# Two row tiles for the 448-deep products, four rotating PSUM bank pairs, and num/den between the halves

## The chip, the cores and the metric

The kernel runs on one core of one Trainium2 chip. The metric is the device time of one execution in microseconds. Executions of one kernel fall into a fast and a slow state; only fast ones are compared. The kernel before took 162.58 us (median of four runs, 162.56 to 162.85).

Names used below: PE is the matmul engine, ACT the scalar engine, DVE the vector engine, POOL the general one, SP the engine that issues most DMAs.

## The reference, cut to what matters

```python
xn  = layernorm(x)                                  # x: 2048 x 448
q, k, v = split(xn @ wqkv)                          # 16 heads of 28
phi = lambda p: concat(softmax(p), softmax(-p))     # p = q or k times w_phi, per head
kv  = einsum(phi(k), v);  z = sum(phi(k))
attn = (phi(q) @ kv) / (phi(q) @ z + 1e-6) @ wo     # "num / den"
ffn  = mish(xn @ w1 + b1) @ w2                      # 448 -> 1792 -> 448
out  = x + attn + ffn
```

Every product with `xn` or the attention output has a contraction of 448 = 7 x 64. The array has 128 rows, so 448 is three and a half passes.

## The kernel before

A 448-deep operand is stored as four chunks of 128 rows that overlap in one 64-row stretch. Of two outputs, each gets three 128-row products (`full`), and then both get their last 64 rows in one go: one output on the array's lower half, the other on the upper half (`rem`, "a half pair").

```python
C0 = (0, 128, 192, 320);  HP = 64;  FULL = ((0, 2, 3), (0, 1, 3))
def full(e, out, lhs, rhs, u, start=True, stop=False):
    for n, c in enumerate(FULL[u]):
        i = e.matmul(out, lhs(ALLP, c), rhs(ALLP, c), start=(start and n == 0), stop=(stop and n == 2))
def rem(e, out, lhs, rhs, u, start=False, stop=True):
    h = slice(HP * u, HP * (u + 1))
    return e.matmul(out, lhs(h, 1 + u), rhs(h, 1 + u), start=start, stop=stop)
```

In the projections one step handles one pair of row tiles (j) and one block of q (i). v alternates between PSUM banks 0-1 and 2-3, k always uses 4-5, q always 6-7, and ACT empties them (`kexp`, `qexp`: two exponentials each, `vevac`: a copy; DVE copies the last two v).

```python
def proj(j, i):
    # v(j): full, full ; q(i): full, full, rem -> qexp ; v(j): rem ; k(j): rem
    # (j == 0: transposes of xn; j == 1: the products that make Wpq)
    # k(j): full, full -> kexp(j), vevac(j)
```

In the FFN stage, two blocks n and n+1 (each 128 columns of w1 for 1024 tokens) share one stretch of half pairs, and num/den products of two token tiles follow it (56 rows deep; no extra step shows between them and half pairs):

```python
for n in range(2 * FC):
    ffn1_full(n, 0); ffn1_full(n, 1)
    ms = [m for m in (n - ND0, n - ND0 + 1) if n % 2 == 0 and 0 <= m < NT]      # ND0 = 8
    if n % 2 == 0:
        ffn1_rem(n)                     # half pairs of n and n + 1
        for m in ms: nd_mm(m)           # num and den on PE, banks 4-5 or 6-7
    mish(n)
    for m in ms: nd(m)                  # five DVE instructions, one POOL product and a small copy
    # ... kv_mm and kvz at n = 0, 2, 4 ; transposes of the attention output
```

The softmax here doesn't subtract the row's maximum and nothing guards it: scores larger than these inputs give would overflow.

## Time and profile before

| what | value | where it is read |
|---|---|---|
| span | 161.0 us | page |
| PE busy, modelled | 95% | page, engines |
| 128-row products, start to start | 216 ns (512 wide), 189 ns (448 wide) | timeline |
| half pairs, start to start | the same 216 and 189 ns | timeline |
| extra per change of array form | about 96 ns, 56 times (54 between 128-row and 64-row forms, 2 from the 56-column kv sums to 128-column products) | timeline |
| ACT per projection step, back to back | 4.37 us | timeline, 25 to 42 us |
| DVE per num/den tile | 1.955 us | timeline, 71 to 97 us |

Columns of the page's first lines: engine, busy us, share of the span, instructions; then one digit for each fortieth of the span, in tenths.

```profile
PE 153.0 (95%) x1317; PEld 75.9 (47%) x1317; DVE 81.8 (51%) x173; ACT 73.2 (45%) x78; POOL 57.4 (36%) x75
...
PE   6999999999799899999999999999999999999992
...
DVE  0877999993449604079999999000051210005211
ACT  3558898999957944655555555620000000000000
```

PE looks full nearly everywhere, which says little: the ends of its matmuls are modelled. The Trainium skill (Perfetto Trace Analysis, Identifying the Most-Contended Engine) says as much, that matmul occupancy is no measure of the distance to the roofline. What counts is from start to start. The next view is the timeline of PE in the FFN stage: start, length, engine, line, operation, output and inputs, array rows x columns, size, count.

```profile
65.02 0.61 PE L348 MATMUL PS<-xnT,W 64*128 64x512 bf16 x4
65.56 2.76 PE L343 MATMUL PS<-xnT,W 128*128 128x512 bf16 x12
68.26 0.60 PE L348 MATMUL PS<-xnT,W 64*128 64x512 bf16 x4
```

Twelve products at 216 ns are 2.59 us, but the half pairs start 2.70 us after the first of the twelve. Two half pairs at 216 ns are 0.43 us, but the twelve start 0.54 us after them. So each change of form costs about 0.1 us. The Trainium skill (TensorEngine Tiling (Array Packing), Key Properties) names the reason: a change of tiling mode drains the engine. It gives no size; this trace does.

The second loss is in the projections. An idle time of the engine stands in brackets with what ended it.

```profile
40.48 1.47 PE L343 MATMUL PS<-xnT,Wpq 128*128 128x512 bf16 x6 [0.42 <-ACT EqT L440]
...
44.31 1.47 PE L343 MATMUL PS<-xnT,Wpq 128*128 128x512 bf16 x6 [0.79 <-ACT EqT L440]
```

q has one bank pair, so these q products wait for the exponentials of the q before. From start to start PE loses 0.58 and 0.96 us here; the brackets show less, since modelled ends overlap the wait.

The third limit is DVE. In the chain of waits (start, length, what), the whole stretch from 69 to 96 us reads like this (steps of 0.02 us named "issue" are left out):

```profile
70.98 0.25 DVE rden L505
71.24 0.12 DVE rq L500
71.38 0.19 DVE rq L501
71.59 0.65 DVE t_1 L503
72.27 0.65 DVE t_1 L504
72.94 0.25 DVE rden L505
```

The last instruction of one tile starts at 70.98 and that of the next at 72.94: DVE needs 1.955 us per token tile, PE with its switches about 1.85.

### The profile page before, as it was taken

How to read it: one execution, taken by the hardware profiler on the slowest of the kernel's cores; microseconds unless marked ns; L12 is line 12 of the kernel's file. 1: busy time of each engine (PE TensorE's matmuls, PEld its weight loads, DVE VectorE, ACT ScalarE, POOL GpSimd, SP SyncE). 2: the span in 40 equal slices, each digit the busy share in tenths (PEclk: the TensorE clock that was granted, in tenths of full speed). 3: DMA queues.
4: the chain of work that ended last, by engine and by line, in shares of the span. 5: the costliest groups of instructions: out<-in, count | busy, mean ns of one | idle time of the engine just before them, and what ended most of it. 6: DMA issues, size and time to landing. Idle time of an engine off the chain costs nothing.

```text
span 161.0 us, 3133 instructions
## 1 busy us (share of the span) xinstructions
PE 153.0 (95%) x1317; PEld 75.9 (47%) x1317; DVE 81.8 (51%) x173; ACT 73.2 (45%) x78; POOL 57.4 (36%) x75
## 2 busy tenths in 40 slices
PE   6999999999799899999999999999999999999992
PEld 6854334443246355344444444455545555545550
DVE  0877999993449604079999999000051210005211
ACT  3558898999957944655555555620000000000000
POOL 6223489977435970026666666300000000000000
PEclk9999999999999999999999999999999999999999
DMA  5995994337910000003336336300022000003010
GB/s 134 328 178 187 280 289 50 67 69 172 372 35 4 0 6 4 0 0 65 69 68 69 66 65 69 65 0 0 0 81 65 29 29 31 4 0 114 29 57 29
DMA packets 24414, 12.79 MB, mean 79 GB/s; under 512 B 17936, under 2 KB 23760, under 8 KB 24400
## 3 DMA queue, kind: packets, MB, share of 16 engines
q1 hardware_dynamic: 23760, 11.65, 30.5%
q10 hardware_dynamic: 608, 0.94, 1.6%
q8 instruction: 10, 0.16, 0.4%
q14 instruction: 4, 0.03, 0.1%
q0 software_dynamic: 32, 0.00, 0.0%
HBM read 6.62 MB, written 1.84 MB: 53 GB/s over the span
## 4 chain that ended last, share of the span: by engine, by line
PE 57%; DVE 24%; ACT 13%; POOL 2%; issue 2%; POOLq 0%; DVEq 0%
PE PS L558 26%; PE PS L343 21%; ACT EqT L440 7%; PE PS L348 4%; ACT hm L419 3%; DVE stats L276 3%; DVE t_0 L504 3%; DVE t_1 L504 3%; DVE t_0 L503 3%; DVE t_1 L503 3%; PE PS L615 2%; DVE rden L505 2%; DVE xn L289 2%; DVE rq L501 2%; ACT v_ext L601 2%
## 5 line engine op out<-in xcount | busy, mean ns | idle before, releaser
L558 PE MATMUL PS<-W,hm 128*128 128x448 bf16 x224 | 44.8, 352 | 0.0
L543 ACT ACTIVATE hm<-PS,b1T 128x1024 bf16<-128x1024 f32 x28 | 31.2, 1113 | 20.9 <-PE PS L343 13.7
L343 PE MATMUL PS<-xnT,W 128*128 128x512 bf16 x168 | 39.0, 380 | 0.6 <-ACT hm L543 0.6
L566 DVE TENSOR_TENSOR out_sb<-PS,x_all 128x448 bf16<-128x448 f32 x16 | 9.4, 621 | 48.8 <-PE PS L348 29.9
L558 PEld LDWEIGHTS PS<-W,hm 128*128 128x128 bf16 x224 | 21.9, 98 | 20.5
L432 POOL TENSOR_TENSOR hm<-hm,rSk 128x1792 bf16<-128x1792 bf16 x8 | 25.6, 3210 | 8.6 <-DVE rSk L431 8.6
L343 PEld LDWEIGHTS PS<-xnT,W 128*128 128x128 bf16 x168 | 15.2, 98 | 19.4 <-issue 1.6
L440 ACT ACTIVATE EqT<-PS 128x1024 bf16<-128x1024 f32 x16 | 15.5, 1021 | 4.6 <-PE PS L348 4.6
L425 DVE TENSOR_REDUCE Sk<-hm 128x64 f32<-128x1792 bf16 x8 | 15.8, 1981 | 0.0
L508 POOL TENSOR_TENSOR o_sb<-t_0,rden 128x504 bf16<-128x504 f32 x8 | 8.3, 1038 | 16.4 <-DVE rden L505 16.4
L419 ACT ACTIVATE hm<-PS 128x896 bf16<-128x896 f32 x16 | 13.9, 927 | 0.3 <-PE PS L343 0.2
L343 PE MATMUL PS<-xnT,Wpq 128*128 128x512 bf16 x48 | 11.7, 379 | 1.2 <-ACT EqT L440 1.2
L343 PE MATMUL PS<-Wo,EqT 128*128 128x448 bf16 x48 | 11.7, 353 | 0.0
L343 PE MATMUL PS<-Wv,xnT 128*128 128x448 bf16 x48 | 10.6, 353 | 0.7 <-DMA xnT<-xn 0.4
L276 DVE BATCH_NORM_STATS2 stats<-x_all 128x6 f32<-128x448 bf16 x16 | 9.3, 616 | 3.7 <-DMA x_all<-in_A_x_dram 3.7
L343 PE MATMUL PS<-Wpk,xnT 128*128 128x448 bf16 x48 | 10.5, 354 | 0.0
L508 POOL TENSOR_TENSOR o_sb<-t_1,rden 128x504 bf16<-128x504 f32 x8 | 8.3, 1039 | 5.3 <-DVE rden L505 5.3
L289 DVE TENSOR_SCALAR xn<-x_all,mv,rstd 128x512 bf16<-128x512 bf16 x16 | 7.3, 497 | 2.4 <-POOL rstd L284 2.3
L348 PE MATMUL PS<-xnT,W 64*128 64x512 bf16 x56 | 8.5, 381 | 0.0
L343 PEld LDWEIGHTS PS<-xnT,Wpq 128*128 128x128 bf16 x48 | 4.5, 98 | 7.0 <-ACT EqT L440 2.1
L343 PEld LDWEIGHTS PS<-Wv,xnT 128*128 128x128 bf16 x48 | 4.2, 98 | 5.5 <-DMA xnT<-xn 0.8
L343 PEld LDWEIGHTS PS<-Wo,EqT 128*128 128x128 bf16 x48 | 4.5, 98 | 4.8 <-issue 0.7
(67 smaller groups left out, 131.7 us busy)
## 6 DMA issues: line engine op xcount, KB each, us to landing
W<-in_B_w_dram SPq DMA_DIRECT2D x2, 896.0 KB, 5.9
out_dram<-out_sb SPq DMA_DIRECT2D x16, 112.0 KB, 1.7
W<-in_B_w_dram SPq DMA_DIRECT2D x1, 1568.0 KB, 7.1
x_all<-in_A_x_dram SPq DMA_DIRECT2D x4, 224.0 KB, 4.4
x_all<-in_A_x_dram ACTq DMA_DIRECT2D x1, 896.0 KB, 5.2
Wv<-in_A_wqkv_dram SPq DMA_DIRECT2D x2, 224.0 KB, 4.5
Wo<-in_A_wo_dram SPq DMA_DIRECT2D x2, 224.0 KB, 6.9
Wk<-in_A_wqkv_dram SPq DMA_DIRECT2D x2, 196.0 KB, 3.6
```

The costliest lines, as they stand in the source:

```text
L276: dve(lambda v: v.bn_stats(stats[:, t, :], x_all[:, t, :]), r=[f"x{t}"], w=[f"st{t}"])
L289: eng(lambda v: v.tensor_scalar(xn[i][:, t % 2, :].rearrange("p (a b) -> p a b", a=2), ap_on(x_all[:, t, 0:1], [[192, 2], [1, 256]]), mv[: ...
L343: i = e.matmul(out, lhs(ALLP, c), rhs(ALLP, c), start=(start and n == 0), stop=(stop and n == 2))
L348: return e.matmul(out, lhs(h, 1 + u), rhs(h, 1 + u), start=start, stop=stop)
L419: act(lambda a, s=s: a.activation(Ek[j % 4][:, :, s, :], PS[:, 4:6, 0:D], ACT.Exp, scale=(1.0 if s == 0 else -1.0)), w=[f"Ek{j % 4}{s}"], ...
L425: dve(lambda v: v.tensor_reduce(Sk[b][:, :], Ek[q][:, :, :, :].rearrange("p t s (h f) -> p (t s h) f", f=DH), AX.X, ALU.add), r=[f"Ek{q}0" ...
L432: pool(lambda g: g.tensor_tensor(phik[:, 2 * j:2 * j + 2, :].rearrange("p t (k f) -> p (t k) f", f=DH), Ek[q][:, :, :, :].rearrange("p t s ...
L440: act(lambda a, s=s: a.activation(EqT[:, s, 2 * gp:2 * gp + 2, tc * 512:(tc + 1) * 512], PS[:, 6:8, :], ACT.Exp, scale=(1.0 if s == 0 else ...
L503: dve(lambda v: v.tensor_tensor(t2v, ps(1, 0, E1), rho, ALU.mult), r=[f"rho{i}"], w=[f"t2{i}"], x=[b, b + 1])
L508: pool(lambda g: g.tensor_tensor(ap_on(ot[:, 0:1], [[KC * P - hh_, 2], [DH, 9], [1, DH]]), ap_on(t1[i][:, 0, 0:1], [[7 * E1, 2], [E1, 9], ...
L543: act(lambda a: a.activation(hm[tcp][:, fc, :].rearrange("p (u n) -> p u n", u=2), PS[:, b:b + 2, :], ACT.Mish, bias=b1T[:, fc:fc + 1]), r ...
L558: i = e.matmul(PS[:, bs[u], cs], hm[q][:, fc, u * P:(u + 1) * P], W2[:, fc, :], start=(u < 4 and fc == 0), stop=(u >= 4 and fc == FC - 1))
```

## The change

The intent is to keep PE in one array mode through the projections, the FFN and the num/den products. Every pair of 448-deep products becomes seven half pairs, except v and k of the first two row tiles, which keep the old form: in half pass `a` output 0 takes the lower half of four chunks while output 1 takes the upper half; in half pass `b` the roles change for the other three. Two row tiles must not write one PSUM bank at the same time (the Trainium skill, TensorEngine Tiling (Array Packing), Gotcha 1: PSUM Pressure), so `b` waits on PE's own semaphore until `a` is done (`fence`), and another block or the num/den products stand between the two.

```diff
+    class Blk:
+        def a(self):
+            def f(e):
+                for c in range(KC):
+                    self.mm(e, 0, LO, c, c == 0, False)
+                    i = self.mm(e, 1, HI, c, c == 0, False)
+                return i
+            self.fence = pe(f, r=self.r, x=self.banks)
+        def b(self):
+            def f(e):
+                for n in range(3):
+                    self.mm(e, 1, LO, (0, 1, 3)[n], False, n == 2)
+                    i = self.mm(e, 0, HI, (0, 2, 3)[n], False, n == 2)
+                return i
+            pe(f, x=self.banks, fence=self.fence)
+            self.done()
+    def two(X, Y):
+        X.a(); Y.a(); X.b(); Y.b()
+    BA, BB, BC, BE = (0, 1), (2, 3), (6, 7), (4, 5)
+    vbank = [BA, BB, BB, BA, BE, BC, BB, BA]
+    kbank = [BE, BE, BC, BB, BA, BE, BC, BB]
+    qbank = [BA, BE, BC, BB, BA, BE, BC, BA]
     ... (v, k, q, FFN and Wo products become Blk; proj, ffn1_full, ffn1_rem, final go)
+    def fbank(n):
+        if n < 6:
+            return (BB, BC, BA)[n % 3]
+        if n < 22:
+            return (BB, BA)[n % 2]
+        return (BE, BB, BA, BC, BE, BB)[n - 22]
     ... (main sequence)
-        if j < 2:
-            wload("SP", W1[:], B_w1, "W1", (j,))
+        if j in (2, 3):
+            wload("SP", W1[:], B_w1, "W1", (j - 2,))
+    two(Q(0), V(2)); two(K(2), Q(1)); two(V(3), K(3)); two(Q(2), V(4)); two(K(4), Q(3))
+    two(V(5), K(5)); two(Q(4), V(6)); two(K(6), Q(5)); two(V(7), K(7)); two(Q(6), Q(7))
     ... (kv_mm(0..3); FF 0,1; kv_mm(4,5); FF 2,3; kv_mm(6,7), kvz; FF 4,5)
+    for n in range(6, 22):
+        X = FF(n)
+        X.a()
+        nd_mm(n - 6)
+        X.b()
+        nd(n - 6)
+        oTr(n - 6)
+    for n in (22, 24, 26):
+        two(FF(n), FF(n + 1))
     ... (last stage: Wo in four groups of half passes, between them the 14 products per tile with W2)
```

More of the change, by code (lines that the diff above doesn't have):

```diff
@@ L51, in __init__, with add @@
         self.dmas = []
-    def add(self, eng, fn, r=(), w=(), x=(), dma=False):
+    def add(self, eng, fn, r=(), w=(), x=(), dma=False, fence=None):
         st = self.streams[eng]
@@ L81, in add @@
                 best[o.eng] = o
+        if fence is not None and known.get(eng, -1) < fence.idx:
+            best[eng] = fence
         for key, o in list(best.items()):
@@ L377, in sl @@
         return lambda h, c: w[h, c, :]
-    VB = (0, 2)
-    def vargs(j, u):
-        t = 2 * j + u
-        return PS[:, VB[j % 2] + u, 0:D], xs(t, 1), sl(Wv)
-    def kargs(j, u):
-        t = 2 * j + u
-        return PS[:, 4 + u, 0:D], xs(t, 1), sl(Wpk)
-    def qargs(i, u):
-        tc, gp = i // 2, i % 2
-        g = 2 * gp + u
-        return PS[:, 6 + u, :], sl(Wpq[:, :, g, :]), xs(4 * tc, 4)
-    def proj(j, i):
-        vb = VB[j % 2]
-        for u in range(2):
-            pe(lambda e, u=u: full(e, *vargs(j, u), u), r=[f"xT{j}"] + wk("Wv"), x=[vb + u])
-        if i is not None:
-            for u in range(2):
-                pe(lambda e, u=u: full(e, *qargs(i, u), u),
-                   r=[f"xT{2 * (i // 2)}", f"xT{2 * (i // 2) + 1}", "Wp000", "Wp001", "Wp010", "Wp011", "Wpq_pad"], x=[6 + u])
-            pe(lambda e: (rem(e, *qargs(i, 0), 0), rem(e, *qargs(i, 1), 1))[1], x=[6, 7])
-            qexp(i // 2, i % 2)
-        pe(lambda e: (rem(e, *vargs(j, 0), 0), rem(e, *vargs(j, 1), 1))[1], x=[vb, vb + 1])
-        pe(lambda e: (rem(e, *kargs(j, 0), 0, True, False), rem(e, *kargs(j, 1), 1, True, False))[1],
-           r=["Wp100", "Wp110"], x=[4, 5])
-        if j == 0:
-            xT_pe(1, act)
-        if j == 1:
-            w_mm(0, 0, 6, dve)
-            w_mm(0, 1, 0, act)
@@ new lines, in _kernel, with __init__, mm @@
+    LO, HI = slice(0, HP), slice(HP, P)
+    class Blk:
+        def __init__(self, outs, lhs, rhs, banks, r, done, start=True, stop=True):
+            self.outs, self.lhs, self.rhs, self.banks, self.r, self.done = outs, lhs, rhs, banks, r, done
+            self.start, self.stop = start, stop
+        def mm(self, e, u, h, c, start, stop):
+            return e.matmul(self.outs[u], self.lhs[u](h, c), self.rhs[u](h, c), start=start and self.start,
+                            stop=stop and self.stop)
+        def a(self):
[13 more added lines that the diff above has]
+            self.done()
@@ new lines, in two, with bk, V @@
+    def two(X, Y):
+        X.a()
+        Y.a()
+        X.b()
+        Y.b()
+    BA, BB, BC, BE = (0, 1), (2, 3), (6, 7), (4, 5)
+    vbank = [BA, BB, BB, BA, BE, BC, BB, BA]
+    kbank = [BE, BE, BC, BB, BA, BE, BC, BB]
+    qbank = [BA, BE, BC, BB, BA, BE, BC, BA]
+    def bk(bs, n):
+        return [PS[:, b, 0:n] for b in bs]
+    def V(j):
+        return Blk(bk(vbank[j], D), [xs(2 * j, 1), xs(2 * j + 1, 1)], [sl(Wv)] * 2, list(vbank[j]),
+                   [f"xT{j}"] + wk("Wv"), lambda: vevac(j))
@@ new lines, in K, with Q @@
+    def K(j):
+        return Blk(bk(kbank[j], D), [xs(2 * j, 1), xs(2 * j + 1, 1)], [sl(Wpk)] * 2, list(kbank[j]),
+                   [f"xT{j}", "Wp100", "Wp110"], lambda: kexp(j))
+    def Q(i):
+        tc, gp = i // 2, i % 2
+        return Blk(bk(qbank[i], 512), [sl(Wpq[:, :, 2 * gp + u, :]) for u in range(2)], [xs(4 * tc, 4)] * 2,
+                   list(qbank[i]), [f"xT{2 * tc}", f"xT{2 * tc + 1}", "Wp000", "Wp001", "Wp010", "Wp011", "Wpq_pad"],
+                   lambda: qexp(tc, gp))
@@ new lines, in first @@
+    def first():
+        vb, kb = vbank[0], kbank[0]
+        va = [(PS[:, vb[u], 0:D], xs(u, 1), sl(Wv)) for u in range(2)]
+        ka = [(PS[:, kb[u], 0:D], xs(u, 1), sl(Wpk)) for u in range(2)]
+        for u in range(2):
+            pe(lambda e, u=u: full(e, *va[u], u), r=["xT0"] + wk("Wv"), x=[vb[u]])
+        pe(lambda e: (rem(e, *va[0], 0), rem(e, *va[1], 1))[1], x=list(vb))
+        vevac(0)
+        pe(lambda e: (rem(e, *ka[0], 0, True, False), rem(e, *ka[1], 1, True, False))[1],
+           r=["Wp100", "Wp110"], x=list(kb))
+        pe(lambda e: e.transpose(PSb[:, 6, 0:FC], b1_rows[0:FC, :], ident[0:FC, 0:FC]), r=["b1r", "ident"], x=[6])
+        xT_pe(1, act)
@@ L412, in proj @@
         for u in range(2):
-            pe(lambda e, u=u: full(e, *kargs(j, u), u, False, True), r=[f"xT{j}", "Wp100", "Wp110"], x=[4 + u])
-        kexp(j)
-        vevac(j)
+            pe(lambda e, u=u: full(e, *ka[u], u, False, True), r=["Wp100", "Wp110"], x=[kb[u]])
+        kexp(0)
     def kexp(j):
+        b = kbank[j]
         for s in range(2):
-            act(lambda a, s=s: a.activation(Ek[j % 4][:, :, s, :], PS[:, 4:6, 0:D], ACT.Exp,
-                                            scale=(1.0 if s == 0 else -1.0)), w=[f"Ek{j % 4}{s}"], x=[4, 5])
+            act(lambda a, s=s: a.activation(Ek[j % 4][:, :, s, :], PS[:, b[0]:b[0] + 2, 0:D], ACT.Exp,
+                                            scale=(1.0 if s == 0 else -1.0)), w=[f"Ek{j % 4}{s}"], x=list(b))
@@ L438, in qexp @@
     def qexp(tc, gp):
+        b = qbank[2 * tc + gp]
         for s in range(2):
             act(lambda a, s=s: a.activation(EqT[:, s, 2 * gp:2 * gp + 2, tc * 512:(tc + 1) * 512],
-                                            PS[:, 6:8, :], ACT.Exp, scale=(1.0 if s == 0 else -1.0)),
-                w=[f"Eq{tc}{gp}{s}"], x=[6, 7])
+                                            PS[:, b[0]:b[0] + 2, :], ACT.Exp, scale=(1.0 if s == 0 else -1.0)),
+                w=[f"Eq{tc}{gp}{s}"], x=list(b))
     def kv_mm(j):
@@ L517, in oTr, with FF @@
         dma_t("SP", oT[:, :, t * P:(t + 1) * P], o_sb[t % NO][:], r=[f"o{t % NO}", f"oa{t % NO}"], w=[f"oT{t}"])
-    def fargs(n, u):
-        tcp, fc = n // FC, n % FC
-        return PS[:, 2 * (n % 2) + u, :], sl(W1[:, :, fc * P:(fc + 1) * P]), xs(8 * tcp + 4 * u, 4)
-    def ffn1_full(n, u):
-        tcp = n // FC
-        first = n % 2 == 0
-        pe(lambda e: full(e, *fargs(n, u), u, first, not first),
-           r=wk("W1") + [f"xT{4 * tcp + 2 * u}", f"xT{4 * tcp + 2 * u + 1}"], x=[2 * (n % 2) + u])
-    def ffn1_rem(n):
-        for i in (n, n + 1):
-            pe(lambda e, i=i: (rem(e, *fargs(i, 0), 0, i > n, i == n), rem(e, *fargs(i, 1), 1, i > n, i == n))[1],
-               r=wk("W1") + [f"xT{4 * (i // FC) + u}" for u in range(4)], x=[2 * (i % 2), 2 * (i % 2) + 1])
+    def fbank(n):
[4 more added lines that the diff above has]
+        return (BE, BB, BA, BC, BE, BB)[n - 22]
+    def FF(n):
+        tcp, fc = n // FC, n % FC
+        b = fbank(n)
+        return Blk(bk(b, 512), [sl(W1[:, :, fc * P:(fc + 1) * P])] * 2, [xs(8 * tcp + 4 * u, 4) for u in range(2)],
+                   list(b), wk("W1") + [f"xT{4 * tcp + u}" for u in range(4)], lambda: mish(n))
     def mish(n):
         tcp, fc = n // FC, n % FC
-        b = 2 * (n % 2)
+        b = fbank(n)
         if tcp:
@@ L542, in mish @@
             rr = [f"Ek{i}{u}" for i in range(4) for u in range(2)]
-        act(lambda a: a.activation(hm[tcp][:, fc, :].rearrange("p (u n) -> p u n", u=2), PS[:, b:b + 2, :], ACT.Mish,
-                                   bias=b1T[:, fc:fc + 1]), r=["b1T"], w=[f"hm{tcp}"] + rr, x=[b, b + 1])
-    OB = [5, 6, 7, 4, 0, 1, 2, 3]
-    def final(q):
-        ts = [8 * q + u for u in range(8)]
-        bs = [OB[u] for u in range(8)]
-        cs = slice(0, D)
-        def wo(u):
-            return PS[:, bs[u], cs], sl(oT[:, :, ts[u] * P:(ts[u] + 1) * P]), sl(Wo)
-        def f1(e, u):
+        act(lambda a: a.activation(hm[tcp][:, fc, :].rearrange("p (u n) -> p u n", u=2), PS[:, b[0]:b[0] + 2, :],
+                                   ACT.Mish, bias=b1T[:, fc:fc + 1]), r=["b1T"], w=[f"hm{tcp}"] + rr, x=list(b))
@@ L557, in f1, with WO, f @@
+    OB = [0, 1, 6, 7, 4, 5, 2, 3]
+    def WO(t, first):
+        bs = [OB[(t + u) % 8] for u in range(2)]
+        return Blk(bk(bs, D), [sl(oT[:, :, (t + u) * P:(t + u + 1) * P]) for u in range(2)], [sl(Wo)] * 2, bs,
+                   [f"oT{t + u}" for u in range(2)] + wk("Wo"), lambda: None, start=first, stop=not first)
+    def f1(t, first):
+        q, u, bank = t // 8, t % 8, OB[t % 8]
+        def f(e):
             for fc in range(FC):
-                i = e.matmul(PS[:, bs[u], cs], hm[q][:, fc, u * P:(u + 1) * P], W2[:, fc, :],
-                             start=(u < 4 and fc == 0), stop=(u >= 4 and fc == FC - 1))
@@ L560, in f1 @@
-            return i
-        def evac(u):
-            t = ts[u]
-            i = t % 4
-            key = f"out{i}"
-            dve(lambda v: v.tensor_tensor(out_sb[i][:, :], PS[:, bs[u], cs], x_all[:, t, :], ALU.add),
-                r=[f"x{t}"], w=[key], x=[bs[u]])
-            dma("SP", ov[:, t, :], out_sb[i][:, :], r=[key])
-        for u in range(4):
-            pe(lambda e, u=u: f1(e, u), r=[f"hm{q}", "W2"], x=[bs[u]])
-            pe(lambda e, u=u: full(e, *wo(u), u % 2, False, False), r=[f"oT{ts[u]}"] + wk("Wo"), x=[bs[u]])
@@ L573, in final @@
-        for v in range(4):
-            pe(lambda e, v=v: [rem(e, *wo(2 * v + u), u, v >= 2, v < 2) for u in range(2)][1],
-               r=[f"oT{ts[2 * v + u]}" for u in range(2)], x=bs[2 * v:2 * v + 2])
-        for u in range(4):
-            evac(u)
-        for u in range(4, 8):
-            pe(lambda e, u=u: full(e, *wo(u), u % 2, False, False), x=[bs[u]])
-            pe(lambda e, u=u: f1(e, u), x=[bs[u]])
-            evac(u)
+                i = e.matmul(PS[:, bank, 0:D], hm[q][:, fc, u * P:(u + 1) * P], W2[:, fc, :],
+                             start=(first and fc == 0), stop=(not first and fc == FC - 1))
@@ L583, in _kernel, with evac @@
+            return i
+        pe(f, r=[f"hm{q}", "W2"], x=[bank])
+    def evac(t):
+        i = t % 4
+        dve(lambda v: v.tensor_tensor(out_sb[i][:, :], PS[:, OB[t % 8], 0:D], x_all[:, t, :], ALU.add),
+            r=[f"x{t}"], w=[f"out{i}"], x=[OB[t % 8]])
+        dma("SP", ov[:, t, :], out_sb[i][:, :], r=[f"out{i}"])
     NP = NT // 2
@@ L594, in vevac @@
     def vevac(j):
-        vb = VB[j % 2]
+        vb = vbank[j]
         out = v_ext[:, 2 * j:2 * j + 2, :, 0:DH]
-        src = PS[:, vb:vb + 2, 0:D].rearrange("p t (h d) -> p t h d", d=DH)
+        src = PS[:, vb[0]:vb[0] + 2, 0:D].rearrange("p t (h d) -> p t h d", d=DH)
         if j >= 6:
-            dve(lambda v: v.tensor_copy(out, src), w=[f"v{j}"], x=[vb, vb + 1])
+            dve(lambda v: v.tensor_copy(out, src), w=[f"v{j}"], x=list(vb))
         else:
-            act(lambda a: a.activation(out, src, ACT.Copy), w=[f"v{j}"], x=[vb, vb + 1])
+            act(lambda a: a.activation(out, src, ACT.Copy), w=[f"v{j}"], x=list(vb))
     def ln_a(j):
@@ L616, in warm @@
            r=["ident"], x=[7])
-    def qlast(i):
-        tc = i // 2
-        for u in range(2):
-            pe(lambda e, u=u: full(e, *qargs(i, u), u),
-               r=[f"xT{2 * tc}", f"xT{2 * tc + 1}", "Wp000", "Wp001", "Wp010", "Wp011", "Wpq_pad"], x=[6 + u])
-        pe(lambda e: (rem(e, *qargs(i, 0), 0), rem(e, *qargs(i, 1), 1))[1], x=[6, 7])
-        qexp(tc, i % 2)
     warm(28)
@@ L642, in _kernel, with after @@
     ln_a(2)
-    for j in range(NP):
-        proj(j, j - 2 if 2 <= j <= 6 else 6 if j == 7 else None)
-        if j == 6:
-            qlast(5)
+    def after(j):
         if j == 0:
+            dve(lambda v: v.tensor_copy(b1T[:], PSb[:, 6, 0:FC]), w=["b1T"], x=[6])
             ln_b(2)
@@ L650, in _kernel @@
             ln_a(3)
-        else:
-            if j >= 2:
-                knorm(j - 2)
-            if j == 1:
-                ln_b(3)
-                xT(3)
-            if j + 3 < NP:
-                ln_a(j + 3)
-            if 1 < j < NP - 2:
-                ln_b(j + 2)
-                xT(j + 2)
-            if j >= 2:
-                knorm2(j - 2)
-        if j < 2:
-            wload("SP", W1[:], B_w1, "W1", (j,))
+            return
+        if j >= 2:
+            knorm(j - 2)
+        if j == 1:
+            ln_b(3)
+            xT(3)
+        if j + 3 < NP:
+            ln_a(j + 3)
+        if 1 < j < NP - 2:
+            ln_b(j + 2)
+            xT(j + 2)
+        if j >= 2:
+            knorm2(j - 2)
+        if j in (2, 3):
+            wload("SP", W1[:], B_w1, "W1", (j - 2,))
         elif j == 5:
@@ L670, in _kernel @@
             masks()
-        if j == 2:
-            pe(lambda e: e.transpose(PSb[:, 3, 0:FC], b1_rows[0:FC, :], ident[0:FC, 0:FC]), r=["b1r", "ident"], x=[3])
-            dve(lambda v: v.tensor_copy(b1T[:], PSb[:, 3, 0:FC]), w=["b1T"], x=[3])
-    ffn1_full(0, 0)
-    ffn1_full(0, 1)
-    qlast(7)
+    first()
+    after(0)
+    V1, K1 = V(1), K(1)
+    V1.a()
+    w_mm(0, 0, 0, dve)
+    w_mm(0, 1, 6, act)
+    K1.a()
+    V1.b()
+    K1.b()
+    after(1)
+    two(Q(0), V(2))
+    after(2)
+    two(K(2), Q(1))
+    two(V(3), K(3))
+    after(3)
+    two(Q(2), V(4))
+    after(4)
+    two(K(4), Q(3))
+    two(V(5), K(5))
+    after(5)
+    two(Q(4), V(6))
+    after(6)
+    two(K(6), Q(5))
+    two(V(7), K(7))
+    after(7)
+    two(Q(6), Q(7))
     knorm(NP - 2)
@@ L680, in _kernel @@
     knorm2(NP - 1)
-    KV_END = 4
-    ND0 = 8
-    for n in range(2 * FC):
-        if n:
-            ffn1_full(n, 0)
-            ffn1_full(n, 1)
-        ms = [m for m in (n - ND0, n - ND0 + 1) if n % 2 == 0 and 0 <= m < NT]
-        if n == 0:
-            for j in range(4):
-                kv_mm(j)
-        if n % 2 == 0:
-            ffn1_rem(n)
-            for m in ms:
-                nd_mm(m)
-        mish(n)
-        for m in ms:
-            nd(m)
-        if n == 2:
-            kv_mm(4)
-            kv_mm(5)
-        if n == KV_END:
-            kv_mm(6)
-            kv_mm(7)
-            kvz()
-        for m in ms:
-            oTr(m)
-    for q in range(2):
-        final(q)
+    for j in range(4):
+        kv_mm(j)
+    two(FF(0), FF(1))
+    kv_mm(4)
+    kv_mm(5)
+    two(FF(2), FF(3))
+    kv_mm(6)
+    kv_mm(7)
+    kvz()
+    two(FF(4), FF(5))
+    for n in range(6, 22):
+        X = FF(n)
+        X.a()
+        nd_mm(n - 6)
+        X.b()
+        nd(n - 6)
+        oTr(n - 6)
+    for n in (22, 24, 26):
+        two(FF(n), FF(n + 1))
+    two(WO(0, True), WO(2, True))
+    for t in range(4):
+        f1(t, False)
+        evac(t)
+    two(WO(4, True), WO(6, True))
+    two(WO(8, True), WO(10, True))
+    for t in range(4, 9):
+        f1(t, False)
+        evac(t)
+    two(WO(12, True), WO(14, True))
+    for t in range(9, 16):
+        f1(t, False)
+        evac(t)
     pr.finish()
```

## The prediction

> **What bounds the kernel now.** Span 161.0 us (162.57 us timed), clock 1.0. The page gives PE 95% busy, but matmul ends are modelled, so I read start-to-start times in the timeline. Full 128-row products follow each other every 216 ns (512 wide) or 189 ns (448 wide); two 64-row products on different halves start 3 ns apart and such pairs follow at the same 216 or 189 ns. Seven half pairs cost what six full products plus one half pair cost: no gain in array time. Removed:
>
> 1. *Mode switches.* Going from 128-row to 64-row products the next start comes 312 ns after the last instead of 216; coming back 308 ns, then 226. About 96 ns per switch, which agrees with the Trainium skill, TensorEngine Tiling (Array Packing), Key Properties: a change of tiling mode drains the engine. The trace holds 56 switches (about 5.3 us). By the new order I count 16; 40 x 0.096 = 3.8 us.
> 2. *Bank waits in the projections.* PE waits 0.58, 0.96 and 0.72 us (at 40.5 and 44.3 on the q exponentials through the single q bank pair, at 55.1 on the Mish), 0.43 us for b1T at 23.0, 0.56 us for an xnT transpose at 17.4. Rotation should remove most: about 2.5 us.
>
> **Added or moved.** A fence on PE's own semaphore between halves: the other block (0.76-0.86 us) or num/den products (0.22 us) between should hide it. The Wpq products now stand before most of V1 and all of K1. They cannot start before 14.8 us (the last WTq load lands at 14.67, DMA issues); about 0.5 us is lost.
>
> **By stage.** Projections: ACT needs 4.37 us per pair of row tiles (0.92+0.90 q, 2x0.80 k, 0.95 v; back to back from 25 to 42), PE 4.17 + 0.19 switch. Both are nearly full, so switches alone gain little; ACT starves from 42 to 51 while PE waits. After: first q exponential near 19.9, then 28.0 us of ACT work, last q product on PE near 46 (was 50.6). FFN blocks 0 and 1 are complete near 51 (was 54.4): -3.4 us.
>
> FFN1: each num/den tile costs DVE 1.955 us against PE 1.85 per tile now; the chain of waits is DVE from 69.1 to 96.4. Switches removed inside this loop gain nothing. But the loop starts after 6.6 blocks instead of 10, at about 60.5 instead of 69.1; six FFN blocks then run at 1.51 us instead of four at 1.62. The phi_k products on POOL (3.21 us each) end near 55.4 and become co-critical for the last kv sums. FFN1 ends near 98.2 (was 104.7). Final stage: 53.4 us either way.
>
> **Predicted:** 161.0 - 6.4 = 154.6 span, 156.2 us; range 153.3 to 159.4. Faster by over 2% (below 159.3) 0.88, within 2% 0.10, slower 0.02.
>
> **What would show it.** Half pairs every 216/189 ns in long runs; no 312 ns steps in FFN1; the q waits gone and ACT continuous from about 20 to 48 us; first num/den near 60 us, DVE still 1.955 us per tile with PE waiting on it; start of the FFN2 products about 6 us earlier, the last 56 us unchanged.
>
> **What would make it wrong.** Half pairs in long runs slower than 216 ns (doubled weight loads not hidden); a fence wait at each half; ACT or the xnT transposes holding PE in the rotated projections; phi_k late, so the kv sums stall and the whole DVE loop moves later. Each costs 1-4 us; only slower pairs could undo the gain.

## The result, and the profile after

The changed kernel took 157.31 us (157.18 to 158.14, four runs) against 162.58. The ratio is 0.9683, with a 95% interval of 0.9648 to 0.9718. A ratio is the mean time of one kernel's fast runs over that of the other's of the same rounds, so it is not quite the ratio of the medians. The predicted 156.2 us is 1.1 us low; the measured time lies inside the stated range.

The page of the changed kernel:

```profile
PE 147.5 (95%) x1665; PEld 75.6 (49%) x1665; DVE 82.3 (53%) x173; ACT 73.1 (47%) x78; POOL 57.4 (37%) x75
...
PE   5887998999999999999999889999999999999992
...
DVE  0877999994699144999999960002210313021221
ACT  3576899999889557655655537700000000000000
```

PE still shows 95%, in a span 5.4 us shorter. The FFN stage in the timeline of PE:

```profile
60.24 0.39 PE L524 MATMUL PS<-KVZ,EqT 56*128 56x60 bf16 x16
60.47 1.88 PE L393 MATMUL PS<-xnT,W 64*128 64x512 bf16 x14
62.18 0.39 PE L524 MATMUL PS<-KVZ,EqT 56*128 56x60 bf16 x16
...
88.01 0.40 PE L524 MATMUL PS<-KVZ,EqT 56*128 56x60 bf16 x16
88.25 0.81 PE L393 MATMUL PS<-xnT,W 64*128 64x512 bf16 x6
89.97 9.24 PE L393 MATMUL PS<-xnT,W 64*128 64x512 bf16 x84 [0.91 <-DVE t L546]
99.04 1.30 PE L393 MATMUL PS<-Wo,EqT 64*128 64x448 bf16 x12
```

The last six blocks are 6 x 7 = 42 half pairs from 89.97 to 99.04 us: 216 ns each. So half pairs keep their pace in long runs, with twice the weight loads, and not one step of 0.1 us is left among them. But the 84 begin with a wait on DVE that the prediction didn't have: from start to start it is 1.07 us.

The projections:

```profile
26.79 0.93 PE L393 MATMUL PS<-Wv,xnT 64*128 64x448 bf16 x8 [0.45 <-DMA xnT<-xn]
...
34.25 1.03 PE L393 MATMUL PS<-xnT,Wpq 64*128 64x512 bf16 x8
35.37 0.93 PE L393 MATMUL PS<-Wv,xnT 64*128 64x448 bf16 x8
```

The waits for q's exponentials are gone; waits for the transposed layernorm output (xnT, by DMA) stand in their place, 0.61 us at 26.8 and 0.25 us at 35.4. The chain of waits from there on:

```profile
30.95 4.38 DMA xnT<-xn
35.33 0.05 issue
35.37 10.65 PE PS L393 x104
```

The span by stages, in us, from the starts of PE's products in the timelines:

| stage | before | after | difference |
|---|---|---|---|
| start to first v product | 8.91 | 8.20 | -0.7 (loads at the start; it varies from run to run) |
| to the end of FFN blocks 0 and 1 | 45.4 | 42.8 | -2.6 |
| to the end of the products with w1 | 50.2 | 48.0 | -2.2 |
| last stage and output | 56.5 | 56.6 | +0.1 |

Summed by start-to-start steps that are too long, PE's switches went from 2.3 to 0.8 us in the second of these stages and its waits from 3.4 to 2.5; in the third the switches went from 2.65 to 0.28 and the waits from 2.3 to 2.6.

### The profile page after: what moved, and what is told of

Read it like the earlier page. It is cut to its first block, busy times and chain, and to the rows that moved or that the text cites. A ratio compares the mean times of both kernels' runs of the same rounds, so it can differ in the third digit from the quotient of the medians.

```text
span 155.6 us, 3834 instructions
## 1 busy us (share of the span) xinstructions
PE 147.5 (95%) x1665; PEld 75.6 (49%) x1665; DVE 82.3 (53%) x173; ACT 73.1 (47%) x78; POOL 57.4 (37%) x75
## 3 DMA queue, kind: packets, MB, share of 16 engines
q1 hardware_dynamic: 23760, 11.65, 32.3%
HBM read 6.62 MB, written 1.84 MB: 54 GB/s over the span
## 4 chain that ended last, share of the span: by engine, by line
PE 57%; DVE 33%; DMA 5%; POOL 2%; issue 2%; DVEq 0%
PE PS L597 27%; PE PS L393 26%; DVE t L545 6%; DVE t L546 6%; DVE stats L278 6%; DVE Sk L466 4%; DVE xn L291 3%; DMA xnT<-xn 3%; PE PS L493 3%; DVE rden L547 2%; POOL rstd L286 2%; DMA x_all<-in_A_x_dram 2%; DVE rq L543 2%; DVE rq L542 1%; DVE mv L281 1%
## 5 line engine op out<-in xcount | busy, mean ns | idle before, releaser
L393 PE MATMUL PS<-xnT,W 64*128 64x512 bf16 x392 | 45.9, 376 | 0.9 <-DVE t L546 0.9
L393 PEld LDWEIGHTS PS<-xnT,W 64*128 64x128 bf16 x392 | 17.5, 94 | 20.3 <-DVE t L546 1.4
L550 POOL TENSOR_TENSOR o_sb<-t,rden 128x504 bf16<-128x504 f32 x16 | 16.6, 1038 | 17.2 <-DVE rden L547 17.2
L393 PE MATMUL PS<-xnT,Wpq 64*128 64x512 bf16 x112 | 14.2, 376 | 0.0
L393 PE MATMUL PS<-Wv,xnT 64*128 64x448 bf16 x98 | 11.6, 350 | 0.5 <-DMA xnT<-xn 0.4
L393 PE MATMUL PS<-Wpk,xnT 64*128 64x448 bf16 x98 | 11.6, 349 | 0.0
L393 PE MATMUL PS<-Wo,EqT 64*128 64x448 bf16 x112 | 11.1, 349 | 0.0
L545 DVE TENSOR_TENSOR t<-PS,rq 128x464 f32<-128x464 f32 x16 | 10.3, 641 | 0.6
L546 DVE TENSOR_TENSOR t<-PS,t 128x464 f32<-128x464 f32 x16 | 10.3, 641 | 0.5
L393 PEld LDWEIGHTS PS<-xnT,Wpq 64*128 64x128 bf16 x112 | 5.4, 94 | 6.0 <-DVE v_ext L624 0.3
```

What stands on the lines that cost most here:

```text
L393: return e.matmul(self.outs[u], self.lhs[u](h, c), self.rhs[u](h, c), start=start and self.start, stop=stop and self.stop)
L545: dve(lambda v: v.tensor_tensor(t2v, ps(1, 0, E1), rho, ALU.mult), r=[f"rho{i}"], w=[f"t2{i}"], x=[b, b + 1])
L546: dve(lambda v: v.tensor_tensor(t1v, ps(0, 0, E1), t2v, ALU.add), r=[f"t2{i}"], w=[f"t1{i}"], x=[b, b + 1])
L550: pool(lambda g: g.tensor_tensor(ap_on(ot[:, 0:1], [[KC * P - hh_, 2], [DH, 9], [1, DH]]), ap_on(t1[i][:, 0, 0:1], [[7 * E1, 2], [E1, 9], ...
```

## The experiments

Twelve runs were made, all with correct results, in four groups on four chips, each group with its own runs of the kernel before. Those gave 162.4 to 163.6 us in the fast state.

### Undo the half passes, keep order and banks

```diff
         def a(self):
-            (four half pairs)
+            for u in range(2):
+                pe(lambda e, u=u: full(e, self.outs[u], self.lhs[u], self.rhs[u], u, self.start, False), ...)
         def b(self):
-            (three half pairs, fence)
+            pe(lambda e: [rem(e, ..., u, False, self.stop) for u in range(2)][1], x=self.banks)
```

> The changed kernel with its order and its bank rotation kept, but each product again as three 128-row products and one 64-row pair. Theory (the switches removed are worth something only where PE bounds): one round trip of about 0.2 us comes back per two blocks; those inside the num/den loop stay hidden under DVE (1.73 + 0.2 us against 1.955), those before 35 us are mostly hidden under the xnT transposes; about 12 round trips count, so 157.3 + 2.4 = 159.7 us (159.0 to 160.5). Rival 1 (the row tiling is immaterial, order and banks gave everything): 157.0 to 157.6. Rival 2 (every switch counts, wherever it stands): about 32 round trips, 163 us or more.

Measured: 160.98, 160.23 and 161.08 us in the fast state, ratio to before 0.9885 (0.9852 to 0.9917).

> The same kernel as e1_full_form (its timed fast runs gave 160.2 to 161.1 us, its profile fell in the slow state), for a profile in the fast state. Theory: 160 to 161 us; inside the num/den loop PE's steps of 0.1 us per switch are there but the loop still turns at DVE's 1.955 us per tile; outside it, about 0.2 us more per two blocks. Rival: the loop turns slower than 1.955 us, so the switches cost there too.

Measured: 160.59 to 160.88 us in the fast state, ratio 0.9876 (0.9832 to 0.9919), and again a slow profile. So a third version left the start of the program (v and k of tile pair 1) in half passes:

> As e1_full_form (order and banks of the changed kernel, products again as 128-row products plus a 64-row pair), but v and k of tile pair 1 keep the half passes, so that the program's start is the changed kernel's and the profile may fall in the fast state (both profiles of e1_full_form fell in the slow one). Time as there, 160.0 to 161.2 us. Theory of the prediction (switches inside the num/den loop stay hidden): the loop turns at 1.955 us per tile. Rival (PE with its switches needs more than DVE, so the loop becomes PE's): 1.98 us or more per tile, no wait of PE on DVE in it, and two thirds of what the full form costs stands in the loop and in the projections, where PE no longer waits for the transposes.

Measured: 161.47 us (161.11 to 161.70), ratio 0.9929 (0.9900 to 0.9957), profile in the fast state. Its FFN loop in the timeline of PE:

```profile
71.17 0.40 PE L535 MATMUL PS<-KVZ,EqT 56*128 56x60 bf16 x16
71.41 0.38 PE L350 MATMUL PS<-xnT,W 64*128 64x512 bf16 x2
71.72 1.47 PE L345 MATMUL PS<-xnT,W 128*128 128x512 bf16 x6
73.12 0.40 PE L535 MATMUL PS<-KVZ,EqT 56*128 56x60 bf16 x16
```

Both "row tiling is immaterial" and "every switch counts" fall; the cost is above the middle theory's 159.0 to 160.5, and the third version's 161.47 us lies a little above its own 160.0 to 161.2. Against the profile of the changed kernel, by stage: first to last q product 29.79 against 28.66 us; from there to the first num/den 15.50 against 14.59; from there to the last FFN product 39.56 against 38.59; then to the last product of all 53.95 against 53.52. That is 3.4 us; another 0.8 us lies before the first q product, where the two differ by a load.

Two parts were under-rated. In the projections the full form has no wait at all for xnT: the switches fill those waits, and cost 1.1 us beyond them. And the loop does turn at 1.95 us per tile, as the theory says, but PE needs that long too, so nothing shows which of the two sets that pace. In the changed kernel PE takes 1.75 us for most of the first eight tiles, until it is ahead of DVE by as much as the bank pairs allow. From the first to the last num/den product of PE it is 27.98 us there and 29.83 us here.

### Undo the rotation of the banks

```diff
-    vbank = [BA, BB, BB, BA, BE, BC, BB, BA]
-    kbank = [BE, BE, BC, BB, BA, BE, BC, BB]
-    qbank = [BA, BE, BC, BB, BA, BE, BC, BA]
+    vbank = [BA, BB, BA, BB, BA, BB, BA, BB]
+    kbank = [BE] * 8
+    qbank = [BC] * 7 + [BA]
```

> The changed kernel with the rotation undone in the projections: v alternates between two bank pairs, k has one, q has one (but for the last q), as in the kernel before. Theory (rotation removes PE's waits on the exponentials): PE waits 0.4 to 0.8 us at nearly every k and q again, 2 to 4 us in all, 159.5 to 161.5 us. Rival (the layernorm and transposes on DVE and DMA pace the projections, so banks don't matter): 157.0 to 157.8.

Measured: 161.43 us (160.91 to 161.92), ratio 0.9925 (0.9890 to 0.9960). The timeline of PE:

```profile
31.70 1.04 PE L393 MATMUL PS<-xnT,Wpq 64*128 64x512 bf16 x8 [0.71 <-ACT EqT L482]
...
35.19 0.93 PE L393 MATMUL PS<-Wpk,xnT 64*128 64x448 bf16 x8 [0.48 <-ACT hm L460]
```

The waits are back: from start to start 0.58 to 0.87 us at six places, 4.5 us together. From the first to the last q product it is 32.3 us against 28.7; every later stage takes as long as in the changed kernel, to 0.03 us. The theory holds. The Trainium skill (Perfetto Trace Analysis, Optimizing Tensor Performance, Matmuls) advises that independent matmul groups rotate through the banks so that emptying one overlaps the next; here it is worth 3.7 us net, since the waits for xnT (0.86 us in the changed kernel) don't show beside the bank waits.

### Only the bank waits, in the kernel before

```diff
+    VBJ = [0, 2, 0, 2, 0, 2, 0, 0]
+    QBJ = [6, 6, 6, 6, 6, 2, 6, 6]
     ... (v(j) in banks VBJ[j], q(i) in banks QBJ[i]; the same for what empties them)
```

> The kernel before with one move: the sixth q product (and with it the last v product) goes to other bank pairs, so the last q products don't wait for the exponentials of the one before. Theory (the two bank waits of 0.58 and 0.96 us at the end of the projections are on PE's critical path): 1.2 to 1.5 us less than before, 161.1 to 161.4 us. Rival (ACT or POOL takes it back before the FFN): 162.3 to 162.7 us.

Measured: 161.18 us (160.97 to 162.05), ratio 0.9924 (0.9898 to 0.9950): 1.2 us, as expected. The two waits of 0.58 and 0.96 us are gone from its trace; before the second of these groups of q products no idle time stands any more (timeline of PE):

```profile
43.60 1.46 PE L343 MATMUL PS<-xnT,Wpq 128*128 128x512 bf16 x6
```

The profiled run is its slowest: there an xnT transpose landed 5.15 us after issue and PE waited 0.87 us for it.

### The num/den loop later

```diff
-    for n in range(6, 22): (num/den tile n - 6 in block n)
-    for n in (22, 24, 26): two(FF(n), FF(n + 1))
+    two(FF(6), FF(7)); two(FF(8), FF(9))
+    for n in range(10, 26): (num/den tile n - 10 in block n)
+    two(FF(26), FF(27))
     ... (bank pairs of the blocks: n < 10 (BB, BC, BA)[n % 3], n < 26 (BA, BB)[n % 2], then BE, BB)
```

> The changed kernel with the num/den loop starting at FFN block 10 in place of 6, with two blocks after it in place of six. The prediction took the earlier start of that loop as a part of the gain: then 3 to 6 us are lost, 160 us or more. Rival (the stage costs PE's work plus what DVE's pace adds inside the loop, wherever the loop stands): 156.3 to 157.7 us, with the loop starting near 66.5 us.

Measured: 158.53 us (158.38 to 159.64), ratio 0.9762 (0.9723 to 0.9801). That is over both the rival's range and the changed kernel's first measurement, and far under the 160 us that the prediction's reading asks for. The timeline of PE shows why it isn't lower:

```profile
66.64 1.04 PE L393 MATMUL PS<-xnT,W 64*128 64x512 bf16 x8 [0.62 <-ACT hm L583]
67.51 0.39 PE L524 MATMUL PS<-KVZ,EqT 56*128 56x60 bf16 x16
```

The first block of the loop waits for the Mish of block 8, because the experiment gave both the same bank pair: 0.78 us from start to start, a flaw of the experiment. From the last q product to the last FFN product this kernel takes 53.98 us and the changed one 53.18. Less that wait it is 53.20. So, with that wait taken off, where the loop stands is worth nothing; the rival's reading holds, though its range was missed.

### The fence with nothing to hide behind

```diff
-    for n in (22, 24, 26):
-        two(FF(n), FF(n + 1))
+    for n in range(22, 28):
+        X = FF(n)
+        X.a()
+        X.b()
```

> The last six FFN blocks of the changed kernel each with its two halves back to back, with no other block between them, so the fence has nothing to hide behind. Theory (a fence costs what the semaphore of a finished half needs to come back, about 0.1 to 0.25 us after its last product could have been followed): 6 x 0.1 to 0.25 = 0.6 to 1.5 us, 157.9 to 158.8 us. Rival (the fence is free anyway, the pairing of blocks is not needed): 157.0 to 157.6.

Measured: 159.53, 159.63 and 159.98 us in the fast state (159.81 is the median with one slow run), ratio 0.9820 (0.9800 to 0.9840). That is above the expected range, but the trace gives the fence itself exactly. The timeline of the weight loads:

```profile
91.84 1.19 PEld L393 LDWEIGHTS PS<-xnT,W 64*128 64x128 bf16 x14 [0.56 <-PE PS L393]
93.59 1.19 PEld L393 LDWEIGHTS PS<-xnT,W 64*128 64x128 bf16 x14 [0.56 <-PE PS L393]
```

A block turns every 1.75 us in place of 1.51. Each of the six shows one start-to-start step that is 226 ns too long: 1.36 us. The other 0.8 us lies in the projections, in code that was not touched: PE waited 1.74 us for the xnT transpose of tile pair 6. That wait was 0.25 us in the changed kernel's first profile and 0.74 us in the one of the late loop.

### The changed kernel again, and the W1 load moved

> The changed kernel itself again, as the reference on this chip for the three that run beside it. 157.0 to 158.2 us. In earlier runs PE's wait for the seventh xnT transpose (before v of tile pair 6) was 0.25, 0.74 and 1.74 us in three profiles whose code was the same up to there; if that wait makes the spread, the time here follows it.

Measured: 158.98, 158.81, 158.73 and 157.37 us, ratio 0.9735 (0.9677 to 0.9794); three of the four lie above the expected range. The profiled run is the one of 158.98, and its timeline has the wait for tile pair 6 at its longest, 1.84 us from start to start:

```profile
37.02 0.93 PE L393 MATMUL PS<-Wv,xnT 64*128 64x448 bf16 x8 [1.68 <-DMA xnT<-xn]
```

Between this profile and the first one of the same kernel the span differs by 1.65 us. This wait is 1.59 us longer, and the first q product starts 0.66 us later because a weight load landed at 14.73 in place of 14.07 us; but the 0.61 us before v of pair 4 is absent here. Beside it ran:

```diff
-        if j in (2, 3):
-            wload("SP", W1[:], B_w1, "W1", (j - 2,))
-        elif j == 5:
+        if j == 5:
+            wload("SP", W1[:], B_w1, "W1")
+        elif j == 7:
             (loads of W2 and Wo)
```

> The changed kernel with the two W1 loads issued after the last xnT transpose and the W2 and Wo loads two tile pairs later. Theory (the W1 loads share the DMA engines with the xnT transposes and make them land 1 to 1.5 us late): transposes land about 3.1 us after issue in place of 4.4 to 4.7, PE's waits before v of tile pairs 4 and 6 (0.6 and 0.25 to 1.7 us) go, 0.5 to 1.2 us less than r_after. Rival (DVE's layernorm sets the pace, and the exponentials follow close behind): within 0.3 us of r_after.

Measured: 157.23 us (157.07 to 157.50), ratio 0.9664 (0.9622 to 0.9707). It is 1.5 us under the kernel beside it, more than expected, but level with that kernel's fastest runs: what it takes away, in these four runs, is the slow part of the spread. By the DMA records, the transposes of tile pairs 5 and 6 land 3.04 and 3.03 us after issue; in the two profiles of the changed kernel it was 4.71 and 4.38, and 3.65 and 5.83. (In the last run below, which moves that load too, it is 3.06 and 3.16.) The wait before v of pair 6 is gone. The half of the theory about pair 4 falls: its transpose still took 4.62 us, with no W1 load under way, and PE waited 0.45 us. What slows that one stays open.

### Another bank pair at the end of the loop

```diff
-        return (BE, BB, BA, BC, BE, BB)[n - 22]
+        return (BB, BE, BA, BC, BE, BB)[n - 22]
```

> The changed kernel with two bank pairs of the last six FFN blocks swapped, so that the first of them does not take the pair from which DVE still reads num/den of tile 14. Theory (the 1.07 us wait at the end of the loop is that bank alone): 0.8 to 1.0 us less than r_after. Rival (the wait only moves to the next block): no gain.

Measured: 156.82 us (156.02 to 157.13), ratio 0.9626 (0.9580 to 0.9672). The 1.95 us under the kernel beside it are not all its own: in its profile the wait for pair 6 is absent, in the other it is 1.84 us. Its own part is read at the place itself. The timeline of PE:

```profile
88.24 0.40 PE L524 MATMUL PS<-KVZ,EqT 56*128 56x60 bf16 x16
88.48 10.09 PE L393 MATMUL PS<-xnT,W 64*128 64x512 bf16 x90
98.41 1.30 PE L393 MATMUL PS<-Wo,EqT 64*128 64x448 bf16 x12
```

From the last num/den product to the last FFN product it takes 9.74 us against 10.61: the wait fell from 1.07 to 0.20 us and did not move elsewhere. So that wait was the bank assignment alone: block 22 had been given the pair from which DVE still reads tile 14.

### Fewer num/den tiles per block

```diff
-    for n in range(6, 22):
+    m = 0
+    for n in range(6, 24):
         X = FF(n)
         X.a()
-        nd_mm(n - 6)
+        if n not in (11, 17): nd_mm(m)
         X.b()
+        ... (nd, oTr and m += 1 under the same condition)
-    for n in (22, 24, 26):
+    for n in (24, 26):
     ... (bank pairs of blocks 24 to 27: BB, BE, BC, BB; the output banks' order swapped to suit)
```

> The changed kernel with the 16 num/den products spread over 18 FFN blocks (two blocks without one), four blocks after the loop, and free bank pairs for these. Theory (inside the loop PE stands still 1.3 us for DVE's pace and 1.07 us for the bank of tile 14, minus two bare fences at 0.23 us): 1.4 to 1.9 us less than the changed kernel, 155.4 to 156.0 us, the loop without a wait of PE. Rival (DVE's 16 x 1.955 us bound the stage whatever PE does): no gain.

Measured: 155.54 us (155.39 to 155.84), ratio 0.9569 (0.9556 to 0.9583), as expected. PE waits nowhere for DVE in the loop; two bare fences of 0.23 us stand in it. The timeline of PE around the first block without a tile, and at the loop's end:

```profile
67.64 0.39 PE L524 MATMUL PS<-KVZ,EqT 56*128 56x60 bf16 x16
67.87 3.43 PE L393 MATMUL PS<-xnT,W 64*128 64x512 bf16 x28
71.14 0.39 PE L524 MATMUL PS<-KVZ,EqT 56*128 56x60 bf16 x16
...
90.62 6.86 PE L393 MATMUL PS<-xnT,W 64*128 64x512 bf16 x62
```

From the first num/den to the last FFN product it takes 36.67 us against 38.59. Of these 1.9 us, 1.07 are the bank wait at the loop's end, which the swapped entry above had already cut by 0.87 us; the other part is 1.3 us of waits for DVE's pace, less the two fences. "DVE bounds the stage" falls: DVE's work need only fit beside PE's.

> The spread num/den products and the late W1 loads together. If the two gains stand in different stages they add: 0.5 to 1.0 us under e4_nd_spread, 154.5 to 155.3 us, and faster than both kernels. Rival (the phi_k products on POOL, which end as the last kv sums begin, take the projections' gain back): as e4_nd_spread.

Measured: 155.34 us (155.13 to 155.85, five runs), ratio 0.9561 (0.9543 to 0.9579). The median lies just above the expected range, and the interval overlaps that of the spread loop alone, so no further gain is shown. The profile tells where it went: the waits for xnT of pairs 4 and 6 are nearly gone (0.05 us), but the transpose of pair 7, now just ahead of the W1 load, landed 4.42 us after issue and PE waits 0.33 us for it. Another 0.36 us passes amid the second group of kv sums, where the profile names no releaser. PE goes on at 51.25 us, and the phi_k products on POOL end at 48.9 and 52.1 us, so it is not shown to be phi_k, as the rival has it. Its last q product starts 0.7 us earlier than that of the spread loop, its last FFN product 0.4 us earlier. Both versions beat the kernel before by 4.3 to 4.4%, and their intervals lie below the changed kernel's.

## Why the prediction was right, and where its sizes were off

**Half pairs keep the pace: right.** 216 ns each in a run of 42 pairs. The trace holds 16 switches, the number that was counted.

**The fence is hidden: right.** No late step stands after the halves where something lies between. Bare, a fence costs 226 ns.

**The bank waits go: right.** They are worth 3.7 us in the new order and 1.2 us in the old one.

**The Wpq products cost something at the start: right, but too small.** 0.5 us was said; PE waited 1.0 us before 14.2 us for the last transposed weight load, and 1.6 us in the repeated run, whose load came 0.66 us later.

**The xnT transposes: named as a risk, left out of the sum.** They cost 0.9 us in the first profile and up to 1.84 us at one place. The wait before pair 6 (none to 1.84 us, by profile) goes when the W1 load leaves that stretch; the one before pair 4 (0.61 us) does not (0.45 us), and its cause stays open.

**First num/den near 60.5 us, phi_k's end near 55.4, DVE at 1.955 us per tile:** measured 60.24, 55.71 and 1.96.

**FFN1 ends near 98.2: 0.8 us off.** Block 22 waits 1.07 us for a bank that DVE still reads. The prediction took the stage as DVE's pace plus six free blocks, and did not follow the bank pairs through the loop's end.

**"But the loop starts after 6.6 blocks instead of 10": the step that failed as a reason.** The prediction listed this as where the FFN stage gains. The late loop shows it to be worth nothing. What the FFN stage gained, by start-to-start steps from the end of block 1 on, is 2.4 us of switches and the bank wait on the first Mish (0.72 us), with the new bank wait taking 1.07 us back; the loop waits for DVE in both kernels, 1.6 and 1.3 us. The end time came out nearly right all the same: the 6.4 us of the prediction are also about what its two listed items, 3.8 us of switches and 2.5 us of bank waits, add up to. Part of the agreement is luck: 0.7 us of the measured 5.4 lie before the first v product, where the prediction had no gain. That product's start ranged from 8.14 to 9.02 us in the profiles of the changed order.

**"Switches removed inside this loop gain nothing": too strong.** In both kernels DVE paces the loop, 1.96 us per tile. But the same 28.0 us from the first to the last num/den product hold 14 FFN blocks before and 15 after. And in the changed kernel's order the full form leaves PE no lead over DVE, and from the first to the last num/den product PE then needs 1.85 us more.

## What to carry to other kernels

Two limits of nearly the same size have to be removed together: here rotation without the half passes gave 1.2 to 2.0 us against the kernel before, half passes without rotation 1.2 us, and both together 5.2 us. The order of the work changed along with them and was not tried alone.

A loop that one engine paces is not a reason to leave it alone: give each turn a little more of the other engine's work and the pace stops mattering (together with the bank at the loop's end 1.9 us here). And after any new bank assignment, follow each pair through the ends of the loops: one swapped entry was worth 0.87 us.

When runs of one kernel differ by more than usual, look for a wait on a DMA whose landing time varies; moving a load that isn't needed yet made the time steadier (157.07 to 157.50 us in four runs, against 157.37 to 158.98 beside them).

## What the Trainium skill lacked or had wrong

- TensorEngine Tiling (Array Packing), Key Properties: it says that a change of tiling mode drains the engine, and gives no size. Here it is about 96 ns each way beyond the normal step (312 ns in place of 216).
- TensorE: Matmul & The Clock Gate, Part 3 (What overlaps and what doesn't): one sentence there says that a weight load overlaps matmuls in flight only when the row group differs, while the paragraph above it also allows a load into the background weight buffer. The trace goes with the paragraph: in the changed kernel the load for one half starts 1 to 2 ns after a product on the same half has started, takes 94 ns, and the products keep their 216 ns. (The halves are told apart by the program's order.) The page's start distance of about 4 ns between row tiles agrees (3 to 4 ns here).
- TensorE: Matmul & The Clock Gate, Back-to-back issue gap: it gives a sustained 131 ns per 512-wide matmul in streams of load and matmul. No stream of 512-wide 128-row products here went under 216 ns, which is what the page calls the isolated gap; half pairs too came every 216 ns.
- TensorE: Matmul & The Clock Gate, the HAM clock gate: it says that about 3.4 us of idle time halves the clock. The two slow profiles of the full form agree in kind: PE stood 4.5 us in the first for a transposed weight load that landed late, the clock row of the profile falls to 5 and 6 tenths in two slices, and 448-wide products then came every 373 ns in place of 189. But the clock fell sooner, 2.6 and 2.9 us after the modelled end of PE's last product before the stand. In the first of these profiles the time lost lies there (the first q product starts 5.0 us later than in the third version); other slow runs were not profiled.
- No page states as one figure the cost of a fence on PE's own semaphore between dependent halves: 226 ns bare after 512-wide products, nothing with 0.22 us of other products between.
